# Gated state-space and dense kernel with all gradients: the second chunk's Y table ahead of the dense steps, Z products and factor fields in another order

## The chip, the cores and the metric

The kernel runs on one core of one Trainium2 chip. The metric is the time of one execution on the device in microseconds. Five engines work side by side, each through its own queue in order: PE (matrix multiply), DVE (vector), ACT (scalar and activation), POOL (general), SP (only issues transfers here). They wait for each other by semaphores. DMA engines move data between DRAM and the on-chip memory (SBUF); PE writes into the PSUM banks, which ACT and DVE read out.

## The reference

A state-space convolution `a` and a two-layer dense network `b` are mixed by a gate `g`; wanted are the mixed output and the gradients of fourteen inputs (all but `B_x`), from a given `grad_out`. L = 2048 positions, D = 448 channels, N = 256 states, F = 1792 hidden units, all bfloat16.

```python
def _A_ref(u, A_re, A_im, B_re, B_im, C_re, C_im, log_dt, Dskip):
    dt = jnp.exp(log_dt)[:, None]
    logdA = dt * (A_re + 1j * A_im)
    dB = dt * (B_re + 1j * B_im)
    P = jnp.exp(logdA[:, :, None] * l[None, None, :])
    K = jnp.einsum("dn,dnl,dn->dl", C_re + 1j * C_im, P, dB).real
    # y = causal convolution of u with K, by FFT of length 2L
    return y + u * Dskip
def _B_ref(x, w1, b1, w2, b2):
    h = jnp.einsum("bsd,df->bsf", x, w1) + b1
    r = jnp.where(h > 0, h, 0)
    return jnp.einsum("bsf,fd->bsd", r * r, w2) + b2
...
g = sigmoid((x * gate_w).sum(-1, keepdims=True))       # x = A_u feeds both branches
out = g * _A_ref(x, ...) + (1 - g) * _B_ref(x, w1, b1, w2, b2)
_out, _vjp = jax.vjp(f, ...);  return (_out, *_vjp(grad_out))
```

## The kernel before, in words

The convolutions are done as two-stage Fourier transforms by matmuls. The prologue (to about 200 us) transforms `u` and the gated gradient, multiplies the spectra and starts the inverse transform that gives the gradient of the convolution kernel K. Powers of the state transition, needed for K and for its gradients, are built for 14 chunks (`NCH`) of 32 channels each and put into a DRAM record per chunk.

**What one chunk needs.** Each power is split in two factors, X (64 values) and Y (41 values), so that K at many positions is a matmul of an X table with a Y table.

- `load_x`, `load_y`: the chunk's record from DRAM, into the tile `F` (X part) and the tile `rec` (Y part, one buffer), issued on POOL. `neg_x` (NX) is a small ACT operation on the X part.
- `fields_y(0..2)` (FY0, FY1, FY2; lines 1044 to 1051): six ACT instructions that spread the record's values into the factor fields that the Y build multiplies by.
- `seeds_y` (YS, line 1059) and `build_y(0..4)` (Y0 to Y4, lines 1018 to 1021): DVE writes the seeds and then three instructions a step until the Y table stands. There is one Y buffer for all chunks. YS also issues the next chunk's `load_y`.
- `kgen` (KM, line 1082) and `k_out` (KO, line 1089): 128 small matmuls of X and Y tables, the chunk's kernel sum, and its copy out of PSUM by ACT.
- `load_yt` (L0, L2 two each, LY all four; line 1106): DMA transposes of the Y table, issued on SP, into a ring of four buffers. For chunk 0 PE turns the table instead (`turn_y`).
- `scale` (SA; SP for the chunk before; ACT, line 1125) and `weigh` (WD; WP; DVE, line 1129): the gradient of K at the chunk's channels, times the position weights. `step_sums` (line 1204) makes it from the inverse transform, via a DRAM buffer.
- `back_z` (Z0 to Z3, lines 1144 and 1150): 32 matmuls with a transposed part of the Y table into one PSUM pair, copied out by ACT.
- `back_p` (P0 after Z0 and Z1, P1 after Z2 and Z3; DVE, line 1159 and 1161) and `back_s` (S, lines 1176 and 1181): products with the X table, and their sums by 128 matmuls, copied out by ACT.
- `tables_x` (X0 to X2; DVE, lines 1008 to 1011): the next chunk's X table. There are two X buffers.

The backward half of chunk c runs one chunk behind its forward half: the tokens Z, P and S at c work on chunk c - 1.

**The dense network** is a generator of steps with a cost each. In its first layer a group is hidden (PE lines 661 and 664, ACT 676), turn (PE 688, ACT 689) and multiply (PE 697, ACT 703). In its second layer `grad_h` makes the hidden gradient (ACT 784), `gate` multiplies it on DVE by the stored hidden activation (line 789; the activation is loaded by `load_r`, lines 772 and 775), and turn, multiply and the turning of weights (765, 766, 811, 813, 814) follow. Two projections (line 905) come last.

**Order.** From line 985 on, the order on every engine is the program's: nothing is reordered. `period(c, tokens)` walks a list of tokens; at each D, dense steps are issued until their summed cost reaches a share of the whole that grows evenly with every D. So the number of Ds sets how much dense work is placed, and a token's place between Ds sets what it stands behind. Stores and loads of the dense part that would overrun buffers are held back and issued at R.

Before `period(0)`, chunk 0's Y table is built, `step_sums` runs, chunk 0's kernel sum is taken and chunk 1's X table is built. `period(0)` then has nine Ds with chunk 1's fields between them; all other tokens are skipped there. `period(1)` does chunk 1's forward and chunk 0's backward half. Chunks 2 to 12 use the list `PERIOD`, and chunk 13 its first part.

Of the kernel before, what the change touches and what calls it, by code (L numbers as in the profile page):

```python
# [20 lines left out]
L, D, N, F = 2048, 448, 256, 1792  # L21
# [298 lines left out]
def kernel(ctx, tc, A_u, A_A_re, A_A_im, A_B_re, A_B_im, A_C_re, A_C_im, A_log_dt, A_Dskip,  # L320
# [4 lines left out]
    V, S, G_, T_ = nc.vector, nc.scalar, nc.gpsimd, nc.tensor  # L325
# [73 lines left out]
    o = 0  # L399
# [549 lines left out]
    def D_(want):  # L949

        while done < total - TAILN and sum(cost[0:done + 1]) <= want:
            N_(1)
# [45 lines left out]
    X2 = 2 * W2  # L998

    def run(base, off, *dims):  # L1000

        return bass.AP(tensor=base.tensor, offset=base.offset + off, ap=[list(base.ap[0])] + [list(d) for d in dims])
# [35 lines left out]
    def seeds_x(c):  # L1038
        V.tensor_copy(run(XW[c % 2][:, 0:1], 0, [2048, 2], [1, 256]), rx_[:, 0:512].rearrange("p (t x) -> p t x", t=2))

    def fields_y(i):

        if i == 0:
            S.mul(PRY.rearrange("p l w t d -> p (l w) (t d)"), run(rec[:, 256:257], 0, [1, 4 * W2], [0, 4]), 1.0)  # L1044
        elif i == 1:
            for t in range(2):
                S.mul(PIY[:, :, :, t].rearrange("p l w d -> p (l w) d"), run(rec[:, 640:641], 0, [1, 4 * W2], [0, 2]), 1.0 - 2.0 * t)  # L1047
        else:
            S.copy(PRZ, run(rec[:, 512:513], 0, [1, W2], [0, 2], [64, 2], [0, 2]))
            for t in range(2):  # L1050
                S.mul(PIZ[:, :, t], run(rec[:, 896:897], 0, [1, W2], [64, 2], [0, 2]), 1.0 - 2.0 * t)
# [22 lines left out]
    def kgen(c):  # L1074
        ps = K.ps("X", [P, CW, NY])
        xb = XW[c % 2][:, 0:1]
        for i in range(CW):
            for h in range(2):
                for t in range(2):
                    for g in range(NG):  # L1080
                        w = h * 32 + g * 8 + i
                        T_.matmul(ps[32 * g:32 * g + 32, i], lhsT=run(xb, 2048 * (1 - t) + w, [W2, 32]), rhs=Y[:, w, t, 0:NY],  # L1082
                                  start=(h == 0 and t == 0), stop=(h == 1 and t == 1), tile_position=(0, 32 * g), skip_group_check=True)
        return ps
# [24 lines left out]
    def turn_y(j, banks):  # L1109

        nonlocal yq
        yt = yring[yq % 4]
        yq += 1
        for h in range(2):
            ps = K.ps(banks[(2 * j + h) % len(banks)], [P, 8, P], bf16)
            for w in range(8):
                T_.transpose(ps[:, w], Y[:, 16 * j + 8 * h + w].rearrange("p t b -> p (t b)"), ident[:])
            (S.copy if h == 0 else V.tensor_copy)(yt[:, 8 * h:8 * h + 8], ps[:])
        return yt
# [75 lines left out]
    def step_sums():  # L1195
        psS = [K.ps(NT[i], [P, 512]) for i in range(4)]
        psE = K.psF()
        tiles = [psS[0], psS[1], psS[2], psS[3], psE[:, 0], psE[:, 1]]
        first, last = {}, {}
        for k, (x8, g, e, gr) in enumerate(ekeys):  # L1200
            first.setdefault((e, gr), k)
            last[e, gr] = k
        for k, (x8, g, e, gr) in enumerate(ekeys):
            T_.matmul(tiles[e][32 * gr:32 * gr + 32, 0:D], lhsT=ct["Ew"][:, 32 * k:32 * k + 32], rhs=hss[x8 // 2][:, g, x8 % 2, :], start=(k == first[e, gr]), stop=(k == last[e, gr]),
                      tile_position=(0, 32 * gr), skip_group_check=True)
        stA, stB = (K.t("st", [P, 4, D], bufs=2) for i in range(2))
        for e in range(6):
            st_ = (stA if e < 4 else stB)[:, e % 4]
            if e == 5:
                st_ = st_[0:1]  # L1210
            S.copy(st_, tiles[e][0:1 if e == 5 else P, 0:D])
            for l in range(2 if e < 2 else 1):
                q = nc.sync if (e + l) % 2 == 0 else G_
                if e < 2:
                    q.dma_start(bass.AP(tensor=dk_d, offset=(32 * e + 16 * l) * D, ap=[[D, 16], [64 * D, 4], [1, D]]), st_[l::2])
                else:
                    q.dma_start(bass.AP(tensor=dk_d, offset=128 * e * D, ap=[[D, 16], [16 * D, 8], [1, D]] if e < 5 else [[D, 1], [1, D]]), st_)
        for cpy in range(2):
            (nc.sync, G_)[cpy].dma_start(DK[64 * cpy + 40:64 * cpy + 41, 0], bass.AP(tensor=dk_d, offset=640 * D, ap=[[D, 1], [1, D]]))
        for x in range(4):  # L1220
            for cpy in range(2):
                (nc.sync, G_)[cpy].dma_start(DK[64 * cpy:64 * cpy + 40, 4 * x:4 * x + 4], bass.AP(tensor=dk_d, offset=x * D, ap=[[16 * D, 40], [4 * D, 4], [1, D]]))
# [43 lines left out]
    neg_x()  # L1266
    YTs[0] = [turn_y(j, NT[0:4]) for j in range(4)]
    seeds_x(1)
    step_sums()
    kps0 = kgen(0)  # L1270
    k_out(0, kps0)
# [15 lines left out]
    br.extend(b[:, 0:7168].rearrange("p (t d) -> p t d", d=D) for b in (KW, DBx))  # L1287
    hold = True
    base, goal = sum(cost[0:done]), sum(cost[0:total - TAILN])
    PERIOD = """YS SA Z0 D R Y0 Y1 D Z1 Y2 D R Z2 Y3 D Z3 Y4 D KM KO LY WD P0 NX D P1 D X0 FY0 S X1 D R FY1 FY2 X2 D""".split()  # L1290
    nd = PERIOD.count("D")

    def token(o, c):

        b = c - 1
        new, nxt, old = c < NCH, c + 1 < NCH, 0 <= b < NCH
        v = int(o[-1]) if o[-1].isdigit() else 0
        if o == "KM" and new:
            kps[0] = kgen(c)
        elif o == "KO" and new:  # L1300
            k_out(c, kps[0])
        elif o == "LY" and new:
            YTs[c] = [load_yt(j) for j in range(4)]
            release()
        elif o == "T":
            YTs[c] = [turn_y(j, NT[0:4] if c > 1 else NT[0:3]) for j in range(4)]
        elif o == "R":
            release()
        elif o[0] == "L" and new:
            YTs.setdefault(c, []).extend(load_yt(v + j) for j in range(2))  # L1310
        elif o == "YS" and new:
            seeds_y()
            if nxt:
                load_y(c + 1)
        elif o == "SA" and new:
            scale(c)
        elif o == "SP":
            scale(b)
        elif o == "WP":
            weigh(b)  # L1320
        elif o == "NX" and nxt:
            neg_x()
        elif o == "WD" and new:
            weigh(c)
        elif o[0] == "X" and nxt:
            tables_x(c + 1, v)
            if v == 2 and c + 2 < NCH:
                load_x(c + 2)
            if v == 2 and c == 9:
                k_store(c)  # L1330
        elif o[0] == "Y" and new:
            build_y(v)
        elif o[0:2] == "FY" and nxt:
            fields_y(v)
        elif o[0] == "Z" and old:
            back_z(b, YTs[b][v], v)
        elif o[0] == "P" and old:
            Qs[b, v] = back_p(b, v)
        elif o == "S" and old:
            for _ in back_s(b, [Qs.pop((b, h)) for h in range(2)]):  # L1340
                pass
    kps = [None]

    def period(c, tokens, k=0):
        for o in tokens:
            if o == "D":
                k += 1
                D_(base + (goal - base) * (c * nd + k) // (nd * NCH - 4))
            elif c or o not in ("YS", "Y0", "Y1", "Y2", "Y3", "Y4", "LY"):
                token(o, c)  # L1350
    period(0, "D D D FY0 D FY1 D FY2 D D D D".split())
    for lb in range(4):
        nc.sync.dma_start(dbt[lb], bass.AP(tensor=DBT_d, offset=lb * P * 2048, ap=[[2048, P], [512, DT], [1, 512]]))
    period(1, "SP YS Y0 D Y1 Y2 WP Z0 D Y3 Y4 Z1 D KM KO Z2 R L0 D Z3 L2 P0 D SA NX P1 D WD X0 FY0 D S X1 D FY1 FY2 D X2 D".split())
    Fx = Fv
    xs = Fx[:, 0:7168].rearrange("p (t d) -> p t d", d=D)
    vp = rounded_positions().reshape(P, LT)
# [29 lines left out]
    for c in range(2, NCH - 1):  # L1387
        period(c, PERIOD)
    G_.dma_start(ct["F1BD"][:, 0:256], nc.inline_tensor(cs["F1K"].astype(ml_dtypes.bfloat16), name="c_F1K").ap())
    i = PERIOD.index("KM")  # L1390
    praw, STs, obs = {}, {}, {}
# [19 lines left out]
    def load_sx(w, q, k, qe=nc.sync):  # L1411
        qe.dma_start(slots[k], bass.AP(tensor=sp_d[w], offset=q * 8 * D, ap=[[16 * 2 * D, P], [1, 8 * D]]))
        return slots[k].rearrange("p (a r d) -> p a r d", a=4, r=2)
# [6 lines left out]
    sx = {(0, q): load_sx(0, q, q - 1) for q in (1, 2)}  # L1420
    period(NCH - 1, [o for o in PERIOD[:i] if o != "SA"])
    D_(goal)
# [271 lines left out]
```

## Time and profile before

| what | value |
|---|---|
| median of 3 runs (lowest to highest) | 767.19 us (760.12 to 768.23) |
| the profiled execution | 767.82 us, of which 766.0 from first to last instruction |
| PE, DVE, ACT, POOL busy | 633.3, 566.3, 511.2, 173.4 us |
| mean granted PE clock | 0.913 of full speed |
| DMA | 177.77 MB, mean 232 GB/s |
| chunk 0's kernel sum copied | 240.0 us |
| last chunk's kernel sum copied | 616.8 us |

The time of an execution is its span plus some 2 us around it. A row of the view in order of time gives start, duration, engine, line, operation, output and inputs, and in brackets the idle time before it and what ended it. "SPq" and "PEld" are SP's queue and PE's weight loads. A row of the waits gives the total in us, the number of times, and the longest. A row of a table by stretch gives busy time of each engine within the stretch, then the granted clock and the DMA share.

### The profile page before, as it was taken

To read this page: it belongs to the slowest core of one execution; us is meant where nothing else is said; L and a number is where in the kernel's file an instruction comes from. 1 tells how busy PE (TensorE), PEld (TensorE's weight loads), DVE (VectorE), ACT (ScalarE), POOL (GpSimd) and SP (SyncE) were. 2 spreads that over 40 slices of the span, in tenths; PEclk is the share of its full clock that TensorE was granted. 3 is DMA by queue.
4 is the path that set the end of the run, shared out by engine and by line. 5 is a ranking of instruction groups with operands and counts; after the bars stand their busy time and mean duration, and the time that the engine had idled before them with its cause. 6 is when DMAs were issued, how large, how long until landed. Compare 5 with 4: busy or idle time off the path is not lost.

```text
span 766.0 us, 20505 instructions
## 1 busy us (share of the span) xinstructions
PE 633.3 (83%) x8597; PEld 339.1 (44%) x8597; DVE 566.3 (74%) x932; ACT 511.2 (67%) x873; POOL 173.4 (23%) x296
## 2 busy tenths in 40 slices
PE   5958969779999876998999997987889968686666
PEld 2412323223446543555664664653555664433211
DVE  1396586674785656898898898884898877859473
ACT  2796958597785756577677767768554534498555
POOL 2252111112173201101211201201100332411553
PEclk9987966889999998899999999999999998899857
DMA  9897586736883998997996977999999976998995
GB/s 200 198 293 244 199 300 243 259 152 231 301 296 105 317 162 195 199 254 207 214 195 210 223 139 195 230 205 217 222 222 218 239 205 203 361 325 304 329 326 149
DMA packets 197116, 177.77 MB, mean 232 GB/s; under 512 B 121534, under 2 KB 174039, under 8 KB 196895
## 3 DMA queue, kind: packets, MB, share of 16 engines
q1 hardware_dynamic: 173823, 113.11, 60.8%
q0 software_dynamic: 15632, 44.48, 19.0%
q10 hardware_dynamic: 7568, 18.88, 6.6%
q8 instruction: 67, 1.10, 0.6%
q14 instruction: 26, 0.21, 0.1%
HBM read 83.95 MB, written 64.32 MB: 194 GB/s over the span
## 4 chain that ended last, share of the span: by engine, by line
PE 41%; DVE 15%; ACT 15%; issue 13%; DMA 12%; POOL 3%; SPq 1%; ACTq 0%; POOLq 0%; DVEq 0%
PE psN L661 5%; PE psN L697 5%; PE psN L905 5%; DMA R<-Y 5%; PE psS L1176 5%; PE psX L1082 4%; DVE Y L1018 3%; DVE Y L1021 3%; DVE F L1019 2%; DMA U<-in_A_u_dram 2%; DMA hd<-F 2%; PE psF L1144 1%; PE psN L688 1%; PE psX L697 1%; ACT P L1150 1%
## 5 line engine op out<-in xcount | busy, mean ns | idle before, releaser
L697 PEld LDWEIGHTS <-U 128*128 128x128 bf16 x448 | 41.0, 100 | 43.5 <-issue 14.0
L1150 ACT CAST P<-psF 128x1024 bf16<-128x1024 f32 x52 | 53.1, 1020 | 8.1 <-PE psF L1144 7.0
L1018 DVE TENSOR_TENSOR Y<-Y,F 128x1024 bf16<-128x1024 bf16 (+3 forms) x70 | 47.9, 685 | 11.1 <-ACT F L1044 7.8
L1019 DVE TENSOR_TENSOR F<-Y,F 128x1024 bf16<-128x1024 bf16 (+3 forms) x70 | 47.3, 676 | 9.5 <-ACT F L1047 9.5
L697 PE MATMUL psN<-S,U 128*128 128x449 bf16 x224 | 49.9, 366 | 0.0
L1021 DVE TENSOR_TENSOR Y<-Y,F 128x1024 bf16<-128x1024 bf16 (+3 forms) x70 | 48.1, 688 | 2.4
L661 PEld LDWEIGHTS <-S 128*128 128x128 bf16 x336 | 30.3, 101 | 43.3 <-issue 16.7
L661 PE MATMUL psN<-S 128*128 128x512 bf16 x168 | 47.5, 410 | 0.6 <-ACT U L676 0.4
L1144 PE MATMUL psF<-S,R 41*128 41x32 bf16 x1664 | 29.5, 174 | 14.6 <-ACT P L1150 12.9
L1144 PEld LDWEIGHTS <-R 41*128 41x128 bf16 x1792 | 27.3, 93 | 26.3 <-issue 23.7
L697 PE MATMUL psX<-D,U 128*128 128x448 bf16 x160 | 37.1, 369 | 1.6 <-ACT D L703 1.6
L689 ACT ACTIVATE U<-psN 128x1024 bf16<-128x1024 bf16 x35 | 36.2, 1034 | 2.4 <-PE psN L688 2.3
L1183 POOL DMA_DIRECT2D s_d<-st x28 | 14.7, 533 | 101.5 <-ACT st L1181 83.4
L676 ACT ACTIVATE U<-psN,b_f 128x512 bf16<-128x512 f32 x48 | 31.1, 688 | 6.1 <-PE psN L664 4.6
L661 PE MATMUL psN<-K,S 128*128 128x512 bf16 x126 | 33.3, 393 | 0.7 <-ACT P L784 0.7
L905 PEld LDWEIGHTS <-U 128*128 128x128 bf16 x252 | 23.7, 99 | 21.9 <-issue 1.8
L296 PEld LDWEIGHTS <-cb_MI 64*128 64x128 bf16 x256 | 15.3, 97 | 31.0 <-issue 22.0
L1059 DVE COPY Y<-rec 128x256 bf16<-128x256 bf16 x14 | 10.4, 740 | 25.0 <-DMA R<-Y 23.1
L905 PE MATMUL psN<-S,U 128*128 128x448 bf16 x140 | 28.4, 353 | 0.0
L1176 PE MATMUL psS<-ident,P 128*64 128x128 bf16 x896 | 27.8, 219 | 0.6 <-issue 0.6
L1176 PEld LDWEIGHTS <-M 128*64 128x64 bf16 x896 | 26.8, 113 | 2.9 <-issue 1.0
L1176 PEld LDWEIGHTS <-P 128*64 128x64 bf16 x896 | 26.0, 110 | 0.8 <-issue 0.7
(417 smaller groups left out, 1695.0 us busy)
## 6 DMA issues: line engine op xcount, KB each, us to landing
sp<-K ACTq DMA_DIRECT2D x8, 896.0 KB, 4.3
rT_d<-U POOLq DMA_DIRECT2D x11, 512.0 KB, 3.0
hd<-F SPq DMA_DIRECT2D x11, 448.0 KB, 13.9
U<-rT_d SPq DMA_DIRECT2D x9, 512.0 KB, 4.6
X<-gd SPq DMA_DIRECT2D x5, 896.0 KB
U<-dhT_d SPq DMA_DIRECT2D x5, 896.0 KB, 6.9
rec_d<-F ACTq DMA_DIRECT2D x2, 1920.0 KB
hd<-st ACTq DMA_DIRECT2D x8, 448.0 KB, 4.7
```

Source lines behind the costliest of these rows:

```text
L661: T_.matmul(pss[k][:], lhsT=w[:, dt], rhs=x(2 * half + k)[:, dt], start=(dt == 0), stop=False, skip_group_check=True)
L676: S.activation(r[:, 512 * lb:512 * lb + 512], pss[k][:], ACT.Relu, bias=b1_f[:, j:j + 1])
L689: S.activation(hn[j % 2][:, 8 * th:8 * th + 8, :], ps[:], f)
L697: T_.matmul(ps[:, 0:w], lhsT=hn[j % 2][:, t, :], rhs=rhs[:, t, :], start=(t == 0), stop=(t == LT - 1))
L905: T_.matmul(ps[:, 0:D], lhsT=src[j][:, P * x:P * x + P], rhs=ws[:, j, :], start=(j == 0), stop=(j == FT - 1))
L1018: V.tensor_tensor(out=run(yb, dst, [64, X2], [d0[1], n // d0[1]], [1, d0[1]]), in0=run(yb, 0, [64, X2], *src), in1=pr, op=ALU.mult)
L1019: V.tensor_tensor(out=run(vb, 0, [n, X2], [d0[1], n // d0[1]], [1, d0[1]]), in0=run(yb, 0, [64, X2], *src), in1=pi, op=ALU.mult)
L1021: return V.tensor_tensor(out=hi, in0=hi, in1=run(vb, n, [2 * n, W2], [-n, 2], [1, n]), op=ALU.add)
L1082: T_.matmul(ps[32 * g:32 * g + 32, i], lhsT=run(xb, 2048 * (1 - t) + w, [W2, 32]), rhs=Y[:, w, t, 0:NY], start=(h == 0 and t == 0), stop=( ...
L1144: T_.matmul(psz[t][:, 32 * b:32 * b + 32], lhsT=yt[64 * t:64 * t + NY, b, :], rhs=DKc[64 * t:64 * t + NY, c % 2, 16 * (j % 2) + b].rearran ...
L1150: S.copy(run(zbs[c, h][:, 0:1], 16 * (j % 2), [1024, 2], [64, NA], [32, 2], [1, 16]), run(psF[:, 0, 0:1], 0, [512, 2], [1, NA], [NA, 2], [ ...
L1176: T_.matmul(sps[64 * h:64 * h + 64, cc, r, :], lhsT=Q[h][r][:, 1024 * t + 64 * a:1024 * t + 64 * a + 64], rhs=(nident if r == 0 and t == 1 ...
```

## The change

Chunk 1's field operations move up to just before `step_sums`. The loop over chunk 1's tokens is cut in two at another place: its seeds and the whole Y build come first, then three Ds, then chunk 0's scale and weigh, chunk 1's kernel sum and chunk 0's Z products with one D between each, then P0. The loads of DBT_d come after eight Ds instead of nine, and chunk 1's transposes right behind them. In `PERIOD`, Z2 and Y3 change places, Z3 moves behind one more D, NX moves one D ahead, and FY1 and FY2 move one D ahead, before X1. The number of Ds in `PERIOD` stays nine.

```diff
@@ -1266,6 +1266,8 @@
     neg_x()
     YTs[0] = [turn_y(j, NT[0:4]) for j in range(4)]
     seeds_x(1)
+    for i in range(3):
+        fields_y(i)
     step_sums()
     kps0 = kgen(0)
     k_out(0, kps0)
@@ -1287,7 +1289,7 @@
     base, goal = sum(cost[0:done]), sum(cost[0:total - TAILN])
-    PERIOD = """YS SA Z0 D R Y0 Y1 D Z1 Y2 D R Z2 Y3 D Z3 Y4 D KM KO LY WD P0 NX D P1 D X0 FY0 S X1 D R FY1 FY2 X2 D""".split()
+    PERIOD = """YS SA Z0 D R Y0 Y1 D Z1 Y2 D R Y3 Z2 D NX Y4 D Z3 KM KO LY WD P0 D P1 D X0 FY0 S FY1 FY2 X1 D R X2 D""".split()
     nd = PERIOD.count("D")
@@ -1346,12 +1348,12 @@
             if o == "D":
                 k += 1
                 D_(base + (goal - base) * (c * nd + k) // (nd * NCH - 4))
-            elif c or o not in ("YS", "Y0", "Y1", "Y2", "Y3", "Y4", "LY"):
+            else:
                 token(o, c)
-    period(0, "D D D FY0 D FY1 D FY2 D D D D".split())
+    period(1, "YS Y0 Y1 Y2 Y3 Y4 D D D SP D WP KM KO D Z0 D Z1 D P0 Z2 D".split(), -nd)
     for lb in range(4):
         nc.sync.dma_start(dbt[lb], bass.AP(tensor=DBT_d, offset=lb * P * 2048, ap=[[2048, P], [512, DT], [1, 512]]))
-    period(1, "SP YS Y0 D Y1 Y2 WP Z0 D Y3 Y4 Z1 D KM KO Z2 R L0 D Z3 L2 P0 D SA NX P1 D WD X0 FY0 D S X1 D FY1 FY2 D X2 D".split())
+    period(1, "L0 Z3 L2 D NX SA P1 D WD X0 FY0 D R S FY1 FY2 X1 D D D X2 D D D D".split())
     Fx = Fv
```

## The prediction, made before the run

> **What bounds the kernel now.** I read the page's busy times first, then the time of each chunk's kernel sum (its copy out of PSUM stands once per chunk, so the copies mark the periods), then busy time by period, then the instructions in order of time where a period is long, and last the waits.
>
> ```profile
> PE 633.3 (83%) x8597; PEld 339.1 (44%) x8597; DVE 566.3 (74%) x932; ACT 511.2 (67%) x873; POOL 173.4 (23%) x296
> ...
> L1089 ACT CAST X<-psX x14: 507/517/523, 240.0 to 616.8; 128x328 bf16<-128x328 f32 x14
> ...
> core 0: us, PE busy (x) PEld busy (x) DVE busy (x) ACT busy (x) POOL busy (x), PEclk, DMA share, GB/s
> 238.00:307.50 69.50, 54.23 (x878) 31.87 (x871) 37.06 (x54) 45.43 (x71) 15.34 (x27) 0.93 0.88 205
> ...
> 309.60:481.70 172.10, 158.20 (x3017) 99.25 (x3017) 152.56 (x214) 126.20 (x221) 26.64 (x46) 0.98 0.89 207
> 481.70:616.80 135.10, 120.08 (x2314) 74.76 (x2313) 113.30 (x159) 80.70 (x114) 18.82 (x33) 0.97 1.12 226
> ```
>
> No engine is full over the whole span. The six steady periods from 309.6 to 481.7 (28.7 us each) are 92% full on PE and 89% on DVE; the five up to 616.8, without the dense work's gates, a little less. The stretch from the first chunk's kernel sum to the third's (238 to 307.5) is another matter: PE works 54.2 of 69.5 us and DVE 37.1. So 15.3 us of PE are free there, and this is the stretch that the change rewrites. What ends the waits in it:
>
> ```profile
> 239.67 0.75 DVE L1059 COPY Y<-rec 128x256 bf16<-128x256 bf16 x1 [0.55 <-PE psX L1082]
> 248.21 0.40 DVE L1018 TENSOR_TENSOR Y<-Y,F 128x256 bf16<-128x256 bf16 x1 [7.79 <-ACT F L1044]
> ...
> 259.25 0.42 DVE L1129 TENSOR_TENSOR S<-S,vw 128x512 bf16<-128x512 bf16 x1 [3.38 <-ACT S L1125]
> 263.51 1.49 PEld L1082 LDWEIGHTS <-R 128*32 128x32 bf16 x93 [0.37 <-issue]
> 266.25 23.10 SPq L1106 DMA_TRANSPOSE R<-Y  x4
> 284.28 0.69 DVE L789 TENSOR_TENSOR P<-P 128x1024 bf16<-128x1024 bf16 x1 [5.53 <-ACT P L784]
> 295.60 0.74 DVE L1059 COPY Y<-rec 128x256 bf16<-128x256 bf16 x1 [7.09 <-DMA R<-Y]
> 307.51 2.05 PE L1082 MATMUL psX<-Y,X 128*32 128x41 bf16 x128 [3.81 <-DVE Y L1021]
> ```
>
> Chunk 1's Y seeds are in place at 239.7, but DVE waits 7.8 us for the factor fields, which ACT makes between dense steps. Chunk 1's kernel sum comes at 263.5 and its Y transposes only at 266.25; these hold SP for 23.1 us. There is one Y buffer, so chunk 2's seeds wait for them until 295.6 (7.1 us of pure DMA wait), the build takes until 307.5, and PE waits 3.8 us for it. The late transposes are what ends last here.
>
> **The change, part by part. 1: the opening.** The six field instructions of chunk 1 move ahead of the step sums. Their prices:
>
> ```profile
> L1044 ACT ACTIVATE F<-rec x14: 1043/1060/1076, 215.5 to 595.1; 128x1024 bf16<-128x1024 bf16 x14
> L1047 ACT ACTIVATE F<-rec x28: 616/632/660, 216.5 to 602.0; 128x512 bf16<-128x512 bf16 x28
> 216.44 0.73 DVE L1059 COPY Y<-rec 128x256 bf16<-128x256 bf16 x1
> 226.78 0.69 DVE L1021 TENSOR_TENSOR Y<-Y,F 128x1024 bf16<-128x1024 bf16 x1
> 237.49 1.84 ACT L1211 CAST st<-psN 128x448 bf16<-128x448 f32 x4 [5.46 <-PE psN L1204]
> 246.92 1.46 PE L661 MATMUL psN<-S 128*128 128x512 bf16 x6
> ```
>
> ACT idles 5.5 us before 237.5, during the step sums, and the fields take at most 1.06 + 5 x 0.63 = 4.2 us (the other five are 512 or 256 elements wide, no more than the L1047 row's), so they cost nothing; without that cover they would cost those 4.2. The whole Y build of chunk 0 ran uninterrupted from 216.44 to 227.47, 11.0 us. Chunk 1's, seeded at 239.67 as now, ends at 250.7 instead of 263.5.
>
> The new order puts chunk 1's kernel sum on PE behind only two of five dense groups (hidden, turn, multiply). The third of them now begins at 246.9 (last row above; from the copy at 240.0 that is some 3.7 us a group), so PE waits 250.7 - 246.9 = 3.8 us: a new wait, with the next hidden matmuls queued behind it. The scaling of chunk 0's sums (L1125) also comes earlier and now waits for its loads:
>
> ```profile
> L1222 POOL DMA_DIRECT2D K<-dk_d x4: 650/666/727, 244.4 to 246.5; - x4
> DMA to landing us min/median/max: 3.7/5.2/6.7
> ```
>
> The last is issued at 246.5 and lands by 251.7 to 253.2. ACT stands still until then, with the copies of a dense result and of the kernel sum behind it. PE is at its kernel sum until 252.8 and then has hidden and turn, two thirds of a group, so this stays covered; at the late end it costs PE under 1 us.
>
> Up to the end of the matmuls for the second gate (283.2 now) both orders have the same PE instructions. A table by stretch gives their work:
>
> ```profile
> 246.90:283.20 36.30, 30.98 (x523) 19.00 (x522) 19.38 (x29) 23.30 (x36) 7.75 (x15) 0.95 1.02 244
> 283.20:307.50 24.30, 14.34 (x202) 7.68 (x202) 15.81 (x23) 15.55 (x24) 2.16 (x4) 0.87 0.86 184
> 300.00:311.00 11.00, 7.19 (x178) 4.52 (x178) 10.76 (x15) 3.79 (x6) 0.54 (x1) 0.55 0.37 75
> ...
> PE psN L765 <- ACT S L766: 1.8, 1, 1.8
> ...
> L1106 SPq DMA_TRANSPOSE R<-Y x48: 1719/2848/11347, 266.3 to 598.3; - x48
> DMA to landing us min/median/max: 5.0/5.0/5.2
> ```
>
> Idle in the first stretch is 5.3 us now. Afterwards I count 3.8 for the kernel sum, about 1 between the first two Z products (one PSUM pair, and a 1.0 us ACT copy), 1.8 where second-layer weights are turned and copied (fourth row), and 0.7 because both gates' matmuls then follow each other in one pair of PSUM banks: 7.3. So the second gate comes 2.0 us later, ending at 287.0 in place of 285.0. But then nothing else is due before chunk 2's seeds. Its X steps now stand before the gates on DVE, and the transposes begin when Z1 and Z3 are done, by my count 258 and 264 (252.8 and a group of 3.7 with two products of 0.6, then the same again and the waits); with the median 2.8 us each and 5 us of landing (last rows) they are in by about 275. Seeds at 287.1 and the 11.9 us that seeds, build and two gates take now (295.6 to 307.5) put chunk 2's kernel sum at 299.0: **8.5 us earlier**. PE's own work gives the same order: 285.2 + 14.3 = 299.5 with part of it at half clock now.
>
> Where the moved transposes go, SP's queue moves too: the four transposes now stand ahead of the first gate's load, three hidden stores and two loads of u. The POOL load of chunk 2's Y record is only issued some 9 us earlier than now, with nobody waiting for it; I price it at nothing.
>
> Bounds: none of the gain above (kernel sum at 307.5) if the transposes keep SP for 23 us and gate loads queue behind; 13 us if PE's idle shrinks from 15.3 to the 3.8 alone (11.5) and the half clock named next goes too. I take 8.5, worked from the rows.
>
> The half clock of 300 to 311 (0.55 in its row) may go, worth about 1.7 us after 307.5, and a similar one may come behind the 3.8 us wait. I put both at zero together. The Trainium skill, page "TensorE: Matmul & The Clock Gate", Part 1, says that an idle window of about 3.4 us drops PE to half rate until a busy window has passed; by that alone the new wait would add some 1.7 us and the sum would be 757.7. The half rate in the row agrees with it, but its onset is no proof of the threshold.
>
> **2: the steady periods.** Three edits: FY1 and FY2 go one dense step forward, right behind the copy of S; NX likewise; Z3 goes one step back, directly before the kernel sum.
>
> ```profile
> DVE Y L1059 <- DMA R<-Y: 16.0, 7, 9.1
> DVE F L1019 <- ACT F L1047: 8.4, 6, 2.1
> DVE M L1159 <- ACT P L1150: 2.6, 2, 1.4
> PE psF L1144 <- ACT P L1150: 11.8, 9, 2.4
> ...
> 377.01 0.74 DVE L1059 COPY Y<-rec 128x256 bf16<-128x256 bf16 x1 [1.30 <-DMA R<-Y]
> 390.20 8.33 SPq L1106 DMA_TRANSPOSE R<-Y  x3
> 390.54 0.56 PE L1144 MATMUL psF<-S,R 41*128 41x32 bf16 x32
> 391.96 1.03 ACT L1150 CAST P<-psF 128x1024 bf16<-128x1024 f32 x1
> 393.02 2.05 PE L1082 MATMUL psX<-Y,R 128*32 128x41 bf16 x128
> 393.45 1.22 DVE L1159 TENSOR_TENSOR M<-P,X 128x2048 bf16<-128x2048 bf16 x1
> ...
> 572.56 6.12 DMA R<-Y
> ```
>
> First the waits from 310 to 617, then one period in order of time, then a piece of the chain that ended last. The field edit takes away up to 8.4 us of DVE waiting, the spreading of Z2 and Z3 part of PE's 11.8; NX is one short ACT instruction, off these lists whichever way, and priced at nothing. Against it stands P1 (L1159). At 393.45 it starts right after Z3's copy (ends 392.99). Z3's matmuls, now at 390.5, would stand just before the kernel sum, at 392.5, and its copy end at 394.0 or a little later: a slip of about 1.0. Where a whole dense group lies between, the slip is up to 3.7. P1 slips with it, then X, then the next seeds; 1.3 us of it fall into the wait for transposes that the seeds have anyway (377.01). A slip of 3.7, less 1.3, less one field wait of 1.4 (8.4/6), costs 1.0 a period; a slip of 1.0 costs nothing and leaves the 1.4 as gain. Over the six periods from 309.6 to 481.7 that is +6 to -8.4, and with a share of the Z waits -10. I take **-3.3**, 0.55 a period, on the gain's side of the middle, since the row shown has the smaller slip. From 482 on, the chain runs through the transposes (last row) and the Y build; both are unchanged, so nothing. The tail from 617 keeps its order.
>
> **Sum:** the profiled execution's 767.8 - 8.5 - 3.3 = **756.0**. The median of the runs shown is 767.2, 0.6 below; the forecast is not shifted for that.
>
> **Rivals.**
> *Opening gain mostly lost (SP's queue).* If the four transposes hold SP as long as now, 258 + 23 = 281, the first gate's load follows.
>
> ```profile
> K<-rT_d SPq DMA_DIRECT2D x5, 256.0 KB, 7.8
> ```
>
> It lands at 289, both gates end at 290.4, and chunk 2's sum comes at 302.3. The u loads behind add some 2 us on the first products of the second layer: 304, a gain of 3. With nothing in the steady periods: **764.8**. For it: the DMA share is 1.02 in that stretch. Against: now the u loads stand ahead of the transposes, afterwards behind.
>
> *Slower: Z3 holds P1.* If Z3 slips by a whole group everywhere and its copy then stands behind one more copy of its kind (1.03 in the row at 391.96), the slip is 4.7 us. Less 2.7 (slack and field wait) that is 2.0 a period, 20 over the ten periods to 592; less 8.5: **779**. It turns slower than before from a slip of 2.7 + 0.85 = 3.55 us on. For it: PE's kernel sum comes 3 us after the Y build here (393.0; the transposes of the finished table start at 390.2), so Z3 is late when P0 is through. Against: when DVE gets later, PE's lag shrinks, and Z3 is ready again.
>
> *More in the periods.* All field waits and part of the Z waits come back, -10 with the opening's 8.5 and 1 us of clock: **748**. For it: the ACT fields stand in PE's chain too. Against: the Y loop: transposes of 8.3 us for three (390.20), with the fourth and the landing some 14, and the 11.0 of the build, leaves little below 25 a period, and the PE work of these periods (158 of 172 us) leaves 2 us each.
>
> **How the numbers follow.** Forecast 0.55, SP's queue 0.20, Z3 slower 0.12, more gain 0.13. The forecast's own range is 750 to 762; from the best steady case to no change: **746 to 768**. One per cent is 7.7 us, about what a measurement here can tell from no change. Below 759.5 lie the third rival and most of the forecast: 0.64; within: 0.23; slower: 0.13.
>
> **What would show it.** Right: chunk 1's Y ends near 251, its kernel sum waits about 4 us, chunk 2's kernel sum starts at 297 to 302, the seeds before it wait for no DMA, and the field waits on L1019 are gone. Wrong: chunk 2's sum beyond 305; a first gate that waits for its load; more DVE waiting before L1159 than 10 us in total; the last kernel sum (616.8 now) not earlier by 8 or more.

## The result, and the profile after

The changed kernel takes 751.93 us (median of 6 runs, 748.57 to 754.02) where the kernel before took 764.49 us beside it. The ratio is 0.9884, with a 95% interval of 0.9835 to 0.9933. Timed again on two other occasions it gave 0.9805 (0.9754 to 0.9856) and 0.9904 (0.9870 to 0.9938). Their mean is 0.986, a gain of about 10 us; singly they stand for 7 to 15 us. Medians are of all runs, while ratios and intervals leave out the runs counted as slow.

First the copies of the chunks' kernel sums out of PSUM and the busy time by stretch; the stretches end at the copies of chunks 2, 8 and 13.

```profile
L1089 ACT CAST X<-psX x14: 502/518/532, 238.5 to 603.4; 128x328 bf16<-128x328 f32 x14
...
236.50:303.50 67.00, 55.59 (x995) 33.25 (x996) 39.66 (x56) 42.47 (x66) 15.23 (x27) 0.92 0.89 215
303.50:470.20 166.70, 153.07 (x2997) 99.14 (x3019) 148.33 (x211) 126.92 (x222) 26.19 (x46) 0.98 0.96 214
470.20:603.40 133.20, 117.24 (x2312) 74.27 (x2311) 115.72 (x162) 80.36 (x113) 18.36 (x33) 0.96 1.12 231
```

From chunk 0's copy to chunk 2's it is 65.0 us (69.6 before), from there to chunk 8's 166.7 (172.1), to the last one 133.3 (135.1). The prologue, though it has chunk 1's six field instructions more, and the unchanged tail are each some 1.5 us shorter. That is no gain of the change: over the fourteen profiles shown or named below, chunk 0's copy comes anywhere from 234.7 to 241.9 us.

The opening, in order of time:

```profile
249.07 2.06 PE L1082 MATMUL psX<-Y,R 128*32 128x41 bf16 x128 [3.55 <-DVE Y L1021]
252.89 1.06 ACT L1125 COPY S<-K 128x512 bf16<-128x512 bf16 x1 [7.23 <-DMA K<-dk_d]
255.07 0.56 PE L1144 MATMUL psF<-S,R 41*128 41x32 bf16 x32
...
284.80 0.73 DVE L1059 COPY Y<-rec 128x256 bf16<-128x256 bf16 x1
288.97 0.75 PE L765 MATMUL psN<-ident,S 128*128 128x128 bf16 x5 [2.92 <-DMA S<-in_B_w_dram]
292.04 0.69 DVE L789 TENSOR_TENSOR F<-F,U 128x1024 bf16<-128x1024 bf16 x1 [4.10 <-DMA U<-rT_d]
300.14 0.69 DVE L1021 TENSOR_TENSOR Y<-Y,F 128x1024 bf16<-128x1024 bf16 x1
301.34 2.05 PE L1082 MATMUL psX<-Y,X 128*32 128x41 bf16 x128
```

Chunk 1's table is ready at 249.0 and its kernel sum waits 3.55 us. Chunk 2's seeds stand behind no transfer any more. But in the middle of chunk 2's build DVE stands 4.1 us at a gate whose hidden rows are still on their way, and PE stands 2.9 us for a second-layer weight. PE then starts chunk 2's kernel sum at 301.34 without a wait, 0.5 us after the table is ready (300.14 + 0.69).

The waits from 300 to 612, DVE and PE:

```profile
DVE Y L1059 <- DMA R<-Y: 15.5, 5, 7.0
DVE M L1159 <- ACT P L1150: 5.7, 2, 5.6
PE psX L1082 <- DVE Y L1021: 10.7, 5, 5.7
PE psF L1144 <- ACT P L1150: 4.5, 6, 1.0
```

DVE's wait for the fields (8.4 us before) is off the list, and PE's waits at Z for ACT's copies are down from 11.8 to 4.5. Its waits for the Y table at the kernel sum grew, from 7.9 to 10.7.

### The profile page after: what moved, and what is told of

It is laid out like the page before. It is cut to its first block, busy times and chain, and to the rows that moved or that the text cites. A ratio compares the mean times of both kernels' runs of the same rounds, so it can differ in the third digit from the quotient of the medians.

```text
span 751.1 us, 20458 instructions
## 1 busy us (share of the span) xinstructions
PE 621.1 (83%) x8556; PEld 337.4 (45%) x8597; DVE 564.7 (75%) x932; ACT 512.1 (68%) x873; POOL 171.6 (23%) x296
## 4 chain that ended last, share of the span: by engine, by line
PE 28%; DMA 12%; DVE 10%; ACT 7%; issue 7%; POOL 1%; SPq 0%; POOLq 0%; ACTq 0%; DVEq 0%
PE psN L905 5%; PE psS L1176 5%; DMA R<-Y 3%; PE psN L661 3%; PE psX L1082 3%; PE psN L697 3%; DVE Y L1021 2%; DVE Y L1018 2%; DVE F L1019 2%; DMA U<-in_A_u_dram 2%; DMA S<-in_B_w_dram 2%; DMA hd<-F 2%; PE psN L296 1%; PE psF L1144 1%; ACT P L1150 1%
## 5 line engine op out<-in xcount | busy, mean ns | idle before, releaser
L697 PE MATMUL psN<-S,U 128*128 128x449 bf16 x224 | 47.8, 355 | 0.2 <-issue 0.2
L661 PE MATMUL psN<-S 128*128 128x512 bf16 x153 | 46.3, 415 | 1.9 <-issue 1.0
L661 PE MATMUL psN<-K,S 128*128 128x512 bf16 x100 | 27.6, 391 | 5.6 <-issue 3.2
```

The source lines that it names most:

```text
L661: T_.matmul(pss[k][:], lhsT=w[:, dt], rhs=x(2 * half + k)[:, dt], start=(dt == 0), stop=False, skip_group_check=True)
L697: T_.matmul(ps[:, 0:w], lhsT=hn[j % 2][:, t, :], rhs=rhs[:, t, :], start=(t == 0), stop=(t == LT - 1))
```

## The experiments

Two theories were open. The prediction's: two gains, most of it in the opening. Its rival: the opening moves slack only, and the gain is the periods'. Each ratio below is against the kernel before on the same occasion.

**The opening alone:** the new early fields and lists for chunk 1, with the old `PERIOD`.

```diff
-    PERIOD = "... R Y3 Z2 D NX Y4 D Z3 KM KO LY WD P0 D P1 D X0 FY0 S FY1 FY2 X1 D R X2 D"
+    PERIOD = "... R Z2 Y3 D Z3 Y4 D KM KO LY WD P0 NX D P1 D X0 FY0 S X1 D R FY1 FY2 X2 D"
```

> The rewritten opening alone: chunk 1's fields and Y build early and the two new lists for chunk 1, with the old PERIOD. Theory (two separate gains that add): chunk 2's kernel sum comes 4 to 5 us earlier after chunk 0's than before (65 us in place of 69.6), as in the profile after the change, the periods to the last kernel sum stay at 307 us, and the time falls by 4 to 6 us, ratio about 0.993 to 0.995. Rival (the opening only moves slack, the later Y loop gives it back): the same early kernel sum, but the last one is no earlier, ratio 0.998 to 1.002. Rival of the prediction's own sizes: 8.5 us, ratio 0.989.

Measured: ratio 1.0003 (0.9970 to 1.0036). The last kernel sum is where it was:

```profile
L1089 ACT CAST X<-psX x14: 502/518/526, 240.1 to 615.7; 128x328 bf16<-128x328 f32 x14
```

Chunk 2's kernel sum came 67.2 us after chunk 0's, the rest to the last took 308.4 (307.2 before). The opening alone is worth nothing that can be measured, as the rival has it. But the kernel sum at 65 us that theory and rival both expected did not come, so it is not shown that a later stage gives something back.

**The new `PERIOD` alone,** with the old opening (the same line the other way round in the kernel before).

> The new PERIOD alone, with the old opening. Theory (separate gains): chunk 2's kernel sum where it was, 69 to 70 us after chunk 0's; from there to the last kernel sum 300 us in place of 307, the DVE waits for FY1 gone; time down by 6 to 8 us, ratio 0.990 to 0.992. Rival (the prediction's size): 3.3 us, ratio 0.9957. Rival (the periods only gain because the opening hands them a chunk with spare time): no gain, ratio 0.998 or more.

Measured: 0.9931 (0.9901 to 0.9961). From chunk 2 to the last kernel sum it took 299.0 us, as the first theory has it. Chunk 2's kernel sum, with the old opening, came after 64.9 us, which neither theory had foreseen: 69.6 had been taken for what the old opening costs.

**The loads of u behind those of the hidden rows.**

```diff
-                    defer(j, load_u)
...
         for j in range(acc.get("r", 0), 3):
             load_r(j)
+        load_u()
```

> The changed kernel with the four loads of u moved behind the loads of the hidden rows 1 and 2 in the SP and POOL queues. In the profile after the change the first gate of hidden tile 1 waits 4.1 us for such a load, in the middle of chunk 2's Y build. Theory (the u loads ahead of it in SP's queue eat the missing 3 to 4 us of the opening): that wait falls under 1 us, chunk 2's kernel sum comes 61 to 62 us after chunk 0's in place of 65, and the time falls 2 to 4 us below the changed kernel (ratio to before 0.984 to 0.986). Rival (the DMA engines are full whatever the order): the wait moves to the second layer's first products with u or stays, ratio as the changed kernel, 0.988.

Measured: 0.9936 (0.9902 to 0.9970), no gain over the changed kernel.

```profile
285.78 0.68 DVE L788 TENSOR_TENSOR F<-F,U 128x1024 bf16<-128x1024 bf16 x1
290.35 0.75 PE L764 MATMUL psN<-ident,S 128*128 128x128 bf16 x5 [6.35 <-DMA S<-in_B_w_dram]
```

This kernel is one line shorter there, so L764 is the L765 of the others. The gate that had waited 4.1 us now waits for no load (first row), and chunk 2's table was ready 61.8 us after chunk 0's kernel sum (62.4 in the changed kernel). But PE's wait for the weight grew from 2.9 to 6.4 us, a later gate waited 4.0 us for ACT's hidden gradient behind it, and PE came to the kernel sum 4.6 us after the table was ready: its copy stands 68.5 us after chunk 0's, where the theory had 61 to 62. So the order of these loads does set the gate's wait, and the wait only moves, as the rival has it. That the DMA engines are full, the rival's reason, is not shown.

**Chunk 1's kernel sum one step later.**

```diff
-"YS Y0 Y1 Y2 Y3 Y4 D D D SP D WP KM KO D Z0 D Z1 D P0 Z2 D"
+"YS Y0 Y1 Y2 Y3 Y4 D D D D SP WP D KM KO D Z0 D Z1 D P0 Z2"
```

> The changed kernel with chunk 1's scale, weigh, kernel sum and Z0 to Z2 one dense step later in the opening. Theory (the 3.55 us that PE waits for chunk 1's Y table at its kernel sum are lost): the wait falls to about 1 us and the gates come 2 us earlier, but gate (1,0) still waits for its load, so chunk 2's kernel sum gains 0 to 1 us and the time is within 1 us of the changed kernel. Rival (PE's wait is what holds the opening): chunk 2's kernel sum 2 to 3 us earlier and the time 2 to 3 us lower, ratio to before 0.985.

Measured: 0.9894 (0.9834 to 0.9955), the changed kernel's time. First this kernel, then the stretch from 245.5 to 262 in it and in the changed kernel:

```profile
250.37 2.05 PE L1082 MATMUL psX<-Y,R 128*32 128x41 bf16 x128 [1.38 <-DVE Y L1021]
255.68 0.47 PE L1144 MATMUL psF<-S,R 41*128 41x32 bf16 x25 [1.64 <-DVE S L1129]
...
245.50:262.00 16.50, 12.52 (x277) 7.79 (x278) 5.60 (x9) 9.75 (x14) 4.01 (x8) 1.00 1.04 263
```

```profile
245.50:262.00 16.50, 12.03 (x268) 7.29 (x270) 6.32 (x9) 7.91 (x12) 2.70 (x6) 0.79 1.14 265
```

The wait fell from 3.55 to 1.38 us, but 1.64 came up at Z0 for the weighted sums. The granted clock of the stretch went from 0.79 to 1.00: the half clock behind the 3.55 us wait is gone with the wait. But it came later instead: from 262 to 270 the clock is 0.79 here and 1.00 in the changed kernel. Chunk 2's kernel sum came after 64.5 us (65.0), and the time did not change beyond its spread, which is too wide to tell the theory's 1 us from the rival's 2 to 3.

**The changed kernel again,** beside kernels with one edit undone.

> The changed kernel once more, timed on one chip beside the kernels with one part of the change undone. The opening alone gave ratio 1.0003 and the new PERIOD alone 0.9931. Theory A (the gain is the periods' alone): ratio 0.992 to 0.994. Theory B (the opening pays once the periods are the new ones): 0.986 to 0.990, below the new PERIOD alone by 2 to 5 us. Chunk 2's Y table is ready 62 to 63 us after chunk 0's kernel sum under both.

Measured: 0.9805 (0.9754 to 0.9856); chunk 2's table at 63.2 us. Taken alone this spoke for theory B. It was timed on another occasion than the new `PERIOD` alone, so it was repeated beside it, below.

**FY1 and FY2 back behind X1 and its step,** all else as changed.

```diff
-S FY1 FY2 X1 D R X2 D
+S X1 D R FY1 FY2 X2 D
```

> The changed kernel with FY1 and FY2 back behind X1 and its D, as before. Theory (the field waits are the periods' gain): the DVE waits of L1019 for L1047 come back with 6 to 9 us from 300 to 610, and the time is 4 to 6 us above the changed kernel. Rival (Z3's place is the gain): no more than 1 us above it, with the DVE waiting again but hidden behind the wait for the transposes.

Measured: 0.9991 (0.9920 to 1.0062), 764.66 us: the whole gain is gone, 12 us beside the changed kernel's 752.30 where the theory had 4 to 6. The waits from 300 to 612:

```profile
DVE M L1159 <- ACT P L1150: 18.6, 7, 6.0
DVE F L1019 <- ACT F L1047: 0.9, 1, 0.9
PE psF L1144 <- ACT P L1150: 9.5, 7, 2.4
```

The theory was right on the edit and wrong on the wait. The field waits did not come back; with Z3 late, DVE waits 18.6 us for Z copies instead, and the fields are ready by the time DVE gets to them.

**Z3 back one step,** all else as changed.

```diff
-NX Y4 D Z3 KM
+NX Z3 Y4 D KM
```

> The changed kernel with Z3 back one step, before Y4 and its D; Z2 and Y3 stay exchanged, NX stays. Theory (fields are the gain, Z3's place costs what P1 waits and returns what PE waits): PE's waits of L1144 for L1150 rise from 4.5 to about 10 us, DVE's of L1159 fall from 5.7 to under 3; time within 2 us of the changed kernel. Rival (Z3 spread over the steps is the gain): 4 to 6 us above the changed kernel. The slower rival of the prediction (Z3 late holds P1): 3 us or more below it.

Measured: 0.9826 (0.9783 to 0.9870) beside 0.9805 for the changed kernel. DVE's waits for Z copies fall to 2.5 us and PE's rise from 4.5 to 6.4 (10 expected). The place of Z3 moves the waits and not the time, as the theory had it.

**The kernel before, a second profile.**

> The kernel before once more, for a second profile. The opening of the first profile had chunk 2's seeds 55.6 us after chunk 0's kernel sum, held 7.1 us by the transposes; the same opening with the new PERIOD had 50.5 and no such wait. Theory (the landing of these transposes varies from one execution to the next, and the first profile had a late one): seeds at 50 to 52 us, wait under 3 us, chunk 2's kernel sum at 65 to 66 us in place of 69.6. Rival (the old PERIOD makes them late, in every execution): 55 to 56 us and 69 to 70 us again.

```profile
293.38 0.74 DVE L1059 COPY Y<-rec 128x256 bf16<-128x256 bf16 x1 [4.51 <-DMA S<-in_B_w_dram]
L1089 ACT CAST X<-psX x14: 505/518/527, 240.1 to 615.1; 128x328 bf16<-128x328 f32 x14
```

Chunk 2's seeds came at 53.3 us, its kernel sum at 67.3: between the two expectations. DVE waited 4.5 us in place of 7.1, and the profile puts the end of that wait down to a weight's load and not to the transposes. The opening was 2.2 us shorter, and most of that was kept: from chunk 0's sum to the last it took 375.0 us, where the first profile took 376.8.

**All on one occasion: the changed kernel, the new `PERIOD` alone, the field edit alone, and stores released earlier.** The third is the kernel before with one edit, the fourth the changed kernel with one:

```diff
-    PERIOD = "... X0 FY0 S X1 D R FY1 FY2 X2 D"
+    PERIOD = "... X0 FY0 S FY1 FY2 X1 D R X2 D"
...
-    period(1, "L0 Z3 L2 D NX SA P1 ...
+    period(1, "R L0 Z3 L2 D NX SA P1 ...
```

> The changed kernel, on the chip on which the new PERIOD alone and the field edit alone are timed beside it. Theory B (the opening pays once the periods are the new ones): 750 to 754 us and 4 to 7 us below the new PERIOD alone. Theory A (the gain is the periods' alone): within 2 us of the new PERIOD alone.

> The new PERIOD with the old opening, again. Theory B: 756 to 760 us; chunk 0's kernel sum to chunk 8's at 231 us or more in the profile, as in its first one (64.9 + 166.3), and the changed kernel at 230 to 232 too, so that the rest of the difference must lie elsewhere. Theory A: 751 to 755 us.

> The kernel before with FY1 and FY2 alone moved ahead of X1; nothing else changed. Undone in the changed kernel, this edit took the whole gain with it (ratio 0.9991), while Z3's place took none (0.9826 with it undone). Theory (the field edit alone makes the periods' gain): as the new PERIOD alone, ratio 0.990 to 0.995, the DVE waits of L1019 for L1047 gone (8.4 us to under 1) and those of L1159 under 4. Rival (it needs NX's or Z2's place as well): half of that or none, 0.996 or more.

> The changed kernel with the held stores of two hidden rows (1 MB) released ahead of chunk 1's transposes, instead of behind them on SP. Theory (the transfers packed behind the transposes make the load for the first gate of hidden tile 1 late, 4.1 us): that wait falls by 2 to 4 us, chunk 2's Y table is ready at 59 to 61 us after chunk 0's kernel sum in place of 62 to 63, time 1 to 3 us below the changed kernel. Rival (the DMA engines are full from 250 to 290 whatever the order): the wait stays at 3 us or more, no change in time.

| kernel | median, us | ratio | interval |
|---|---|---|---|
| changed kernel | 755.36 | 0.9904 | 0.9870 to 0.9938 |
| new `PERIOD` alone | 757.48 | 0.9898 | 0.9862 to 0.9934 |
| field edit alone | 754.75 | 0.9861 | 0.9798 to 0.9923 |
| changed, stores released earlier | 753.74 | 0.9888 | 0.9845 to 0.9931 |

Theory A holds: side by side, the changed kernel, its `PERIOD` alone and the field edit alone cannot be told apart. The absolute times fitted neither theory: 755.36 lies above theory B's 750 to 754 for the changed kernel, 757.48 above theory A's 751 to 755 for the new `PERIOD`. What decides is the distance between the two, 2.1 us by the medians and 0.0006 by the ratios, where theory B had 4 to 7 us.

The second profile of the new `PERIOD` alone warns against reading too much from one execution: chunk 0's copy came at 234.7, chunk 8's 234.5 us later (230.8 in the changed kernel beside it), and chunk 2's sum to the last took 304.9 us, not 299.0.

The field edit alone, its copies and its waits from 300 to 612:

```profile
L1089 ACT CAST X<-psX x14: 499/519/525, 239.9 to 605.3; 128x328 bf16<-128x328 f32 x14
...
PE psF L1144 <- ACT P L1150: 6.4, 8, 1.2
DVE M L1159 <- ACT P L1150: 1.1, 1, 1.1
```

The last kernel sum stands at 605.3 where the kernel before has 616.8. The wait of DVE for the fields is off this list too, and PE's at Z is nearly halved although no Z has moved. Why, one period shows: the two FY1 instructions now start right behind the copy of S (371.50 + 0.59), where the kernel before had them at 378.0, after the copies of a product and of turned weights, and so later in the queue that leads to ACT's scale and Z0 copy. First rows of the kernel before, then those of the field edit alone:

```profile
377.12 0.54 ACT L805 CAST D<-psN 128x449 bf16<-128x449 f32 x1 [1.03 <-PE psN L697]
378.02 1.16 ACT L1047 ACTIVATE F<-rec 128x512 bf16<-128x512 bf16 x2
```

```profile
371.50 0.59 ACT L1181 COPY st<-psS 128x512 f32<-128x512 f32 x1 [1.34 <-PE psS L1176]
371.98 1.15 ACT L1047 ACTIVATE F<-rec 128x512 bf16<-128x512 bf16 x2
374.17 0.52 ACT L805 CAST D<-psN 128x449 bf16<-128x449 f32 x1
```

Behind the copy of S, ACT had idled 1.03 us until PE's dense product was there to be copied (L805). With the fields in that place it no longer idles before L805; its 1.34 us ahead of the copy of S, while PE does the sums, are unchanged. So the fields fill ACT time in which its next dense copy is not yet due, and no longer stand between the dense copies and Z0's copy, for which PE waits.

From the copy of S to the start of Z0's copy it is 7.5 us before and 6.5 here. The other periods agree: added up over the eleven of this stretch, ACT takes 107.3 us from FY0 to Z0's copy in the kernel before, 95.2 with the field edit alone, 96.5 in the changed kernel, and 107.5 with FY1 and FY2 back. Over all fourteen profiles, chunk 2's kernel sum to the last takes 307.2 to 308.4 us in the four that have FY1 and FY2 at the old place, and 297.0 to 304.9 us in the ten that have them moved.

With the stores released earlier the gate's wait fell and chunk 2's table was ready at 60.2 us:

```profile
DVE F L789 <- DMA U<-rT_d: 1.6, 1, 1.6
PE psX L1082 <- DVE Y L1021: 3.6, 1, 3.6
PE psN L765 <- DMA S<-in_B_w_dram: 3.0, 1, 3.0
```

That is the theory's 2 to 4 us; but the kernel sum still came after 66.2 us, since PE got there no sooner, 3.9 us after the table was ready. PE keeps its own waits in the opening (the last two rows: the new kernel-sum wait and the weight); how much of its lateness each makes is not shown. No time was gained.

## Why the prediction was right in its total and wrong in its split

**The total** (756.0 forecast, 751.9 measured) was right, and that was luck. It was made of -8.5 for the opening and -3.3 for the periods; the runs show near 0 and about -9. Two errors of opposite sign, some 8 us too much and some 6 too little, nearly cancelled.

**What bounds the opening** was the step that failed first. "The late transposes are what ends last here" was read from one execution. Chunk 0's to chunk 2's kernel sum took 69.6, 67.3, 64.9, 67.1 and 64.8 us in the five profiles with the old opening, and 65.0, 66.3, 66.1, 67.2, 65.2 and 66.1 in the six with the changed opening (the changed kernel three times, the opening alone, FY back, Z3 back). The means are 66.7 and 66.0. The profile that the prediction stood on had the longest of the eleven. Chunk 2's build already follows `PERIOD`, so like should be held against like: with the old `PERIOD` it is 69.6 and 67.3 us with the old opening and 67.2 with the changed one; with the new `PERIOD`, 64.9 and 67.1 against 65.0, 66.3 and 66.1.

**The early fields and Y build** went as worked out: chunk 1's table came at 249.0 on a clock that started 1.5 us earlier (250.7 forecast), the new wait was 3.55 us (3.8), and the scale waited for its loads until 252.9, or 254.5 on the clock before, somewhat past the 251.7 to 253.2 given. That stayed cheap, as forecast: PE had no wait behind it here, and 0.7 us in the changed kernel's second profile.

**The opening's sum** held up to the second gate and failed behind it, in "nothing else is due before chunk 2's seeds" and in PE's 299.5, which adds PE's work without any idle time. These rows are from the changed kernel:

```profile
245.50:283.00 37.50, 30.64 (x519) 18.57 (x523) 16.76 (x23) 22.13 (x34) 8.04 (x16) 0.91 1.06 252
283.00:301.00 18.00, 13.61 (x182) 7.23 (x184) 12.43 (x20) 12.12 (x18) 1.07 (x2) 0.91 0.74 209
```

Up to 283 PE idles 6.9 us, where 7.3 were counted, and chunk 2's seeds came as forecast (46.3 us after chunk 0's copy; 287.1 - 240.0 = 47.1). Then the build took 16 us in place of 11.9, 4.1 of it for the gate's load, and PE idled 4.4 us, 2.9 of it for the weight.

PE is what ended last: in eight of the nine profiles with the changed opening it reached chunk 2's kernel sum 0.5 to 4.6 us after the table was ready. The kernel sum's start at 301.3 lies within the 297 to 302 given as a sign, but only on the earlier clock; on the clock before it is 302.9. The wait for the weight is 2.9 to 6.4 us in all nine and in none of the five with the old opening, where PE waited 2.2 us there for an ACT copy. Its load goes out at 279.2, behind the turning of the first weights, and lands 9.7 us later, while PE is free for it at 286.1. In the kernel before, those weights were turned from 272.4 and not from 277.0, the load went out at 274.1, and PE came for it at 288.4. The first rival named SP's queue, and it was half right: a load was late, though for a later gate than the first, and the transposes held SP for 13.3 us and not for 23.

**The half clock** was put at zero. It did appear behind the wait (0.79 in the changed kernel's stretch, 1.00 where the wait was 1.38), as the Trainium skill's "TensorE: Matmul & The Clock Gate", Part 1, has it, and the one of 300 to 311 went, with a shorter one (3.4 us from 289.0) in its place. That one stands behind the 2.9 us wait for the weight, which is shorter than the window of about 3.4 us that this page of the Trainium skill names, so the runs show a half clock behind shorter waits too. Both signs were there; what they are worth together is not shown, since the kernel with the shorter wait only moved its half clock to a later place.

**The field edit** was mis-sized: "up to 8.4 us of DVE waiting", of which 3.3 net was taken; the third rival, with 10 us in the periods, had their size. From chunk 2's kernel sum to the last it is 307.2, 307.7 and 308.4 us with the old `PERIOD` and 300.0, 297.0 and 298.4 in the changed kernel: -9.3 by the means. Nearly all of it falls before chunk 8's copy (172.1, 176.0 and 171.4 us against 166.7, 163.8 and 164.7); behind it the prediction's "nothing" holds (135.1, 131.7 and 137.0 against 133.2, 133.2 and 133.7). What was missing was ACT's own queue: the fields stood ahead of Z0's copy, and part of PE's 11.8 us of waiting at Z was theirs.

**Z3's slip** was there (DVE waits of 5.7 us at P1 in the changed kernel, 2.6 before), under the 10 us given as the limit, and was absorbed. With FY1 and FY2 late as well it rose to 18.6 us. So the mechanism of the slower rival exists, and in these runs it is large only with ACT late; even then the kernel was not measurably slower than before (0.9991).

## What to carry to other kernels

Look for work that stands in an engine's queue ahead of what another engine waits for, and for a stretch where that engine is idle anyway: moving five small ACT instructions by one step was worth more than rebuilding the longest gap. A gap with one late transfer in it, read from one execution, should be seen in a second one before it is priced. And when a stretch has several things due at nearly the same time (a load, a gate, a weight), taking away the latest gains only the distance to the next.

## What was not expected of the hardware

One and the same kernel took 69.6 and then 67.3 us for the opening, another 64.9 and then 67.1; with the old opening chunk 2's seeds, which stand behind chunk 1's transposes, came 50.5 to 55.6 us after chunk 0's copy, with the changed one 45.9 to 47.0. What makes a landing late is not settled. The three waits of 3.55 to 3.57 us on PE in the changed kernel's three profiles each had a half clock behind them (3.4 or 6.8 us long), while a wait of 1.38 us left the clock at 1.00 to 262 us.
